# Pairing the half-empty last tiles of two batches, and splitting the first attention block, in a fused attention and MLP-mixer kernel

## The chip, the cores and the metric

The kernel runs on one core of one Trainium2 chip. The metric is the device time of one execution in microseconds (us). Each kernel was executed several times. All executions named here count as fast ones, that is within 1.5% of the fastest of their kernel. A profiled execution also has a span, from its first to its last instruction. It is about 1.8 us shorter than the time of the same execution. Where two traces are compared below, spans are meant. The granted clock is the share of its full speed at which TensorE was clocked, as the profile records it.

Five engines work side by side: PE is TensorE (PEld its weight loads), DVE is VectorE, ACT is ScalarE, POOL is GpSimd and SP is SyncE.

## The reference

There are B = 8 batches of S = 3008 rows. The width D is 256, z is 64 wide, the token layer has 256 hidden units and the channel layer 1536.

```python
# attention with a gate
scores = (1 / S) * z @ z.transpose(0, 2, 1)
x = u * (np.maximum(scores, 0) ** 2 @ v)
# MLP mixer on x: over tokens, then over channels
h  = np.maximum(x.transpose(0, 2, 1) @ w_tok1, 0) @ w_tok2
u2 = x + h.transpose(0, 2, 1)
out = u2 + np.maximum(u2 @ w_ch1, 0) @ w_ch2
```

3008 rows are 23 tiles of 128 rows and one of 64. That last half tile, one in each batch, is what the first part of the change is about.

## The kernel before

A Python program decides the order of the instructions while it builds the kernel. It keeps a model of each engine's time and fills TensorE with pieces of four kinds: score runs (`sc`, z by z), attention blocks (`acc`, squared scores by v), and the heads (`a_ps`, `h_ps`) and tails (`hp`, `op`) of the mixer of the batch before. ScalarE and VectorE empty the accumulators. GpSimd issues the loads of u, v and later z. SyncE issues the transposing DMAs and the stores.

The last layer of the mixer, with the narrow tile, is:

```python
def ch2(q, half, i, end):
    ...
    n = full_tiles[q]
    rows = [P if half * 2 + j < n else TAIL for j in range(2)]   # P = 128, TAIL = 64
    c0 = (half * 2 + i) * P
    for cc in range(CHT):                                        # CHT = 12
        nc.tensor.matmul(
            op[:rows[i], i, :], st["h2", q, cc // 2][:, cc % 2, c0:c0 + rows[i]],
            w_ch2_sb[:, cc, :], start=(cc == 0 and i == 0), stop=(cc == CHT - 1),
            skip_group_check=True)
```

An attention block goes in two halves, each four tiles of keys long, one for each half of the width of v:

```python
def do_half(start, g):
    ...
    dh = blk.half
    count = GK - 1 if g == LAST else GK                          # GK = 4
    start, end = on_pe(start, "full", count * column_time(blk.W))
    for i in range(count):
        av_matmul(blk, g, i, dh, final and i == count - 1)
```

The start loads v chunk 0, then lets GpSimd wait for a late z chunk (`mark`) before it asks for the other v chunks. It turns the first z chunks by matmuls with the identity (`zp`), with matmuls of zeros (`fill`) between them:

```python
load_v(0, 0)
...
nc.gpsimd.tensor_copy(mark[:], zf0[NG - 2][:, 0, :1])
for c in range(1, NG):
    load_v(0, c)
...
fill(6)
for c in range(DT):                     # DT = 2: chunks 0 and 1 on TensorE
    zp = psum.tile([P, GK, P], F32, tag=f"acc{c}", name=f"zp{c}", bufs=1)
    turn_on_pe(double_first_z(c), zp)
    nc.scalar.copy(zTs[0][:, c * GK:c * GK + GK, :], zp[:])
for c in range(DT, GK):                 # chunks 2 and 3 by a transposing DMA
    turn_z(zf0[c], zTs[0], c, nc.vector, "h2", 8)
fill(2)
```

Chunks 4 and 5 are turned later, inside the first block, and ScalarE copies them out.

## Time and profile before

| what | value |
|---|---|
| time, median of 4 runs | 1179.82 us (1178.64 to 1181.26) |
| span of the profiled run | 1179.6 us |
| first matmul starts | 1.2 us |
| first gate of the first block (first `xT<-acc` on VectorE) | 23.95 us |
| last matmul ends | 1175.50 us |
| last matmul to the end of the span | 4.09 us |
| waits of TensorE for a DMA between gate and last matmul | two: 2.08 us at 250 us (`x_sb`), 0.27 us at 491 us (`zT`) |

The prediction was made when three of these four runs were known; their median was 1179.19. It shows the lines of this profile. The last four rows cut the span into three stretches: the start up to the first gate, the middle, which is one stream of matmuls, and the end after the last matmul.

### The profile page before, as it was taken

To read this page: it belongs to the slowest core of one execution; us is meant where nothing else is said; L and a number is where in the kernel's file an instruction comes from. 1 tells how busy PE (TensorE), PEld (TensorE's weight loads), DVE (VectorE), ACT (ScalarE), POOL (GpSimd) and SP (SyncE) were. 2 spreads that over 40 slices of the span, in tenths; PEclk is the share of its full clock that TensorE was granted. 3 is DMA by queue.
4 is the path that set the end of the run, shared out by engine and by line. 5 is a ranking of instruction groups with operands and counts; after the bars stand their busy time and mean duration, and the time that the engine had idled before them with its cause. 6 is when DMAs were issued, how large, how long until landed. Compare 5 with 4: busy or idle time off the path is not lost.

```text
span 1179.6 us, 17778 instructions
## 1 busy us (share of the span) xinstructions
PE 1164.1 (99%) x7023; PEld 635.6 (54%) x7123; DVE 552.0 (47%) x831; ACT 527.7 (45%) x657; POOL 146.8 (12%) x272
## 2 busy tenths in 40 slices
PE   9999999999999999999999999999999999999998
PEld 3334555545546545565555645565454655555666
DVE  5776655245442554434634255233743255412444
ACT  7885644336343453434534345343643345423221
POOL 2561101100121010110101101100201000000000
PEclk9999999999999999999999999999999999999999
DMA  8998957999799985998859977797978989542122
GB/s 147 168 154 138 178 100 134 163 132 164 115 157 172 152 154 107 184 166 147 143 112 184 160 136 131 147 181 136 155 133 144 180 126 165 114 90 63 52 81 61
DMA packets 462339, 162.95 MB, mean 138 GB/s; under 512 B 426224, under 2 KB 439856, under 8 KB 462256
## 3 DMA queue, kind: packets, MB, share of 16 engines
q1 hardware_dynamic: 434400, 129.12, 58.9%
q0 software_dynamic: 27344, 32.32, 20.0%
q8 instruction: 55, 0.90, 0.3%
q10 hardware_dynamic: 512, 0.38, 0.1%
q14 instruction: 28, 0.23, 0.1%
HBM read 65.40 MB, written 24.64 MB: 76 GB/s over the span
## 4 chain that ended last, share of the span: by engine, by line
PE 95%; DMA 2%; issue 1%; SPq 1%; ACT 1%; DVE 1%; POOL 0%; DVEq 0%; POOLq 0%; ACTq 0%
PE acc L497 40%; PE op L708 21%; PE hp L677 20%; PE sc L374 7%; PE a_ps L630 3%; PE h_ps L647 3%; DMA zT<-zr 1%; ACT at L410 1%; DMA x_sb<-xT 1%; PE wp L143 1%; DVE xT L653 0%; SPq L449 0%; SPq L456 0%; POOL zr L111 0%; PE zp L135 0%
## 5 line engine op out<-in xcount | busy, mean ns | idle before, releaser
L410 ACT ACTIVATE at<-sc 128x1024 bf16<-128x1024 f32 (+1 forms) x294 | 281.0, 1022 | 180.0 <-PE sc L374 178.4
L497 PE MATMUL acc<-at,v_sb 128*128 128x512 bf16 (+2 forms) x1474 | 356.1, 378 | 2.4 <-issue 1.0
L497 PEld LDWEIGHTS <-v_sb 128*128 128x128 bf16 (+1 forms) x2304 | 209.0, 98 | 266.4 <-issue 66.0
L690 ACT ACTIVATE h2pre<-hp 128x1024 bf16<-128x1024 f32 (+1 forms) x186 | 186.3, 1006 | 350.5 <-PE hp L677 349.5
L418 DVE TENSOR_TENSOR at<-at 128x1024 bf16<-128x1024 bf16 (+1 forms) x294 | 206.2, 708 | 181.7 <-ACT at L410 181.1
L708 PE MATMUL op<-w_ch_sb,h2pre 128*128 128x256 bf16 (+1 forms) x2304 | 270.3, 273 | 0.1
L677 PE MATMUL hp<-xT,w_ch_sb 128*128 128x512 bf16 (+1 forms) x1118 | 264.1, 374 | 2.2 <-DVE xT L653 0.4
L708 PEld LDWEIGHTS <-h2pre 128*128 128x128 bf16 (+1 forms) x2304 | 225.7, 98 | 48.7 <-issue 1.8
L497 PE MATMUL acc<-fl,v_sb 128*128 128x512 bf16 (+1 forms) x772 | 186.6, 370 | 1.8 <-issue 0.8
L677 PEld LDWEIGHTS <-w_ch_sb 128*128 128x128 bf16 x1152 | 112.4, 98 | 128.3 <-issue 1.9
L721 DVE TENSOR_TENSOR res<-op,u_sb 128x512 f32<-128x512 f32 x88 | 60.9, 692 | 237.5 <-PE op L708 237.1
L692 DVE TENSOR_SCALAR h2pre<-hp 128x1024 bf16<-128x1024 f32 (+1 forms) x102 | 123.0, 1206 | 49.0 <-PE hp L677 48.6
L586 DVE TENSOR_TENSOR xT<-acc,uT 128x512 bf16<-128x512 f32 (+1 forms) x96 | 63.4, 665 | 79.5 <-PE acc L497 79.1
L374 PE MATMUL sc<-zT 64*128 64x512 bf16 (+1 forms) x752 | 97.6, 360 | 0.7 <-DMA zT<-zr 0.3
L398 ACT ACTIVATE at<-sc 128x512 bf16<-128x512 f32 (+3 forms) x164 | 59.4, 446 | 63.7 <-PE sc L374 63.6
L160 POOL DMA_DIRECT2D ur<-in_u_dram x48 | 26.2, 545 | 360.0 <-DMA uT<-ur 360.0
L437 DVE TENSOR_TENSOR at<-at 128x512 bf16<-128x512 bf16 (+3 forms) x164 | 46.0, 333 | 44.3 <-ACT at L398 44.3
L111 POOL COPY zr<-zs 128x512 bf16<-128x512 bf16 x42 | 29.1, 694 | 288.1 <-DMA zT<-zr 287.5
L374 PEld LDWEIGHTS <-zT 64*128 64x128 bf16 x752 | 32.1, 94 | 58.2 <-issue 40.3
L653 DVE TENSOR_TENSOR xT<-xT,h_ps 128x1024 bf16<-128x1024 bf16 (+1 forms) x48 | 55.7, 1191 | 12.2 <-PE h_ps L647 12.2
L149 POOL DMA_DIRECT2D v_sb<-in_v_dram x48 | 26.0, 546 | 186.2 <-PE acc L497 186.1
L630 PE MATMUL a_ps<-x_sb,w_tok_sb 128*128 128x256 bf16 x384 | 44.5, 273 | 2.1 <-DMA x_sb<-xT 2.1
(37 smaller groups left out, 202.0 us busy)
## 6 DMA issues: line engine op xcount, KB each, us to landing
out_dram<-res SPq DMA_DIRECT2D x88, 256.0 KB, 2.3
v_sb<-in_v_dram POOLq DMA_DIRECT2D x40, 256.0 KB, 5.2
ur<-in_u_dram POOLq DMA_DIRECT2D x40, 256.0 KB, 5.6
zs<-in_z_dram POOLq DMA_DIRECT2D x35, 64.0 KB, 4.4
at<-at SPq DMA_TRANSPOSE x123, 2.8
fl<-at SPq DMA_TRANSPOSE x100, 4.6
v_sb<-in_v_dram POOLq DMA_DIRECT2D x8, 192.0 KB, 7.1
w_ch_sb<-in_moe_w_ch_dram POOLq DMA_DIRECT2D x4, 384.0 KB, 5.3
```

The lines of the kernel that those rows point to most:

```text
L374: nc.tensor.matmul(sc[:, r, c0:c1], zT[h, k * P:(k + 1) * P], zT[h, q * QW + c0:q * QW + c1], start=True, stop=True)
L398: nc.scalar.activation(a3[:, i, c0:c1], sc[:, r, c0:c1], ACT.Relu, scale=inv_S)
L410: nc.scalar.activation(view, sv, ACT.Relu, scale=inv_S)
L418: nc.vector.tensor_mul(view, view, view)
L497: nc.tensor.matmul(o, vs[blk.b, g][rows, i, dh * P:(dh + 1) * P], rhs, start=first, stop=stop, skip_group_check=True)
L586: nc.vector.tensor_mul(xT[:, dh, :full * P].rearrange("p (t s) -> p t s", s=P), acc[:, :full * P].rearrange("p (t s) -> p t s", s=P), uT[: ...
L630: nc.tensor.matmul(st["a_ps"][:, th, :], w_tok1_sb[:, k, th * P:(th + 1) * P], x[:, :, i, :], start=(k == 0 and th == 0), stop=(k == KT - ...
L677: nc.tensor.matmul(hp[:, r, :W], w_ch1_sb[:, dc, cc * P:(cc + 1) * P], xT[:, dc, :W], start=(dc == 0), stop=(dc == DT - 1))
L690: nc.scalar.activation(h2[:, :, :W], hp[:, :, :W], ACT.Relu)
L692: nc.vector.tensor_single_scalar(h2[:, :, :W], hp[:, :, :W], 0.0, AX.max)
L708: nc.tensor.matmul(op[:rows[i], i, :], st["h2", q, cc // 2][:, cc % 2, c0:c0 + rows[i]], w_ch2_sb[:, cc, :], start=(cc == 0 and i == 0), s ...
L721: nc.vector.tensor_add(res.rearrange("p i (h d) -> p i h d", d=P), op.rearrange("p i (h d) -> p i h d", d=P), us[:, :, half * 2:half * 2 + ...
```

## The change

The intent is to save TensorE time in two places.

- **Pairs of tails.** The last 64 rows of an even batch wait, as columns of the tile `hs`, for the last 64 rows of the odd batch after it. GpSimd copies both there. One full matmul group then serves both.
- **Start.** The first score run waits for one turned z chunk instead of two. The first two blocks run by half blocks, so that v matmuls can begin when two of the four tiles of `at` are ready. Score runs in the first block may be short when ScalarE would run dry (`starved`). The copies of the late z chunks move from ScalarE to VectorE.

The last batch does its pair tile before its last full tiles (`halves`), so that three adds and three small stores are not at the very end. The core of the diff, with cuts at "...":

```diff
+    def grain(b, q, g):
+        return 2 if b + q == 0 and g < 2 else GK
...
-        dh = blk.half
-        count = GK - 1 if g == LAST else GK
-        start, end = on_pe(start, "full", count * column_time(blk.W))
-        for i in range(count):
-            av_matmul(blk, g, i, dh, final and i == count - 1)
+        dh, tiles = blk.steps[blk.half]
+        start, end = on_pe(start, "full", len(tiles) * column_time(blk.W))
+        for i in tiles:
+            av_matmul(blk, g, i, dh, final and i == tiles[-1])
...
+                if q == NQ - 1:
+                    if c2 == 0 and b % 2 == 0:
+                        pair["hs"] = sb.tile([P, CHT, P], BF16, tag="hs", name="hs", bufs=1)
+                    r = b % 2 * TAIL
+                    nc.gpsimd.tensor_copy(
+                        pair["hs"][:, 2 * c2:2 * c2 + 2, r:r + TAIL], h2[:, :, W - TAIL:W])
...
+            both = half * 2 + i == n
...
+                if both:
+                    h2 = pair["hs"][:, cc, :]
+                else:
+                    h2 = st["h2", q, cc // 2][:, cc % 2, c0:c0 + P]
                 nc.tensor.matmul(
-                    op[:rows[i], i, :], st["h2", q, cc // 2][:, cc % 2, c0:c0 + rows[i]],
-                    w_ch2_sb[:, cc, :], start=(cc == 0 and i == 0), stop=(cc == CHT - 1),
-                    skip_group_check=True)
+                    op[:, i, :], h2, w_ch2_sb[:, cc, :], start=(cc == 0 and i == 0),
+                    stop=(cc == CHT - 1), skip_group_check=True)
...
+        def halves(q):
+            return (1, 0) if (b, q) == (B - 1, NQ - 1) else (0, 1)
+        def pieces_of(q, half):
+            return 1 if q == NQ - 1 and half == 1 and b % 2 == 0 else 2
...
-            "act", end + 0.1, 0.52, 0.66,
-            lambda t: nc.scalar.copy(zTs[0][:, c * GK:c * GK + GK, :], zp[:]),
+            "dve", end + 0.1, 0.66, 0.8,
+            lambda t: nc.vector.tensor_copy(zTs[0][:, c * GK:c * GK + GK, :], zp[:]),
...
-    fill(6)
+    fill(7)
...
-    fill(2)
+    fill(1)
...
+    score_run(units[:2], 5.3)
...
+        elif (starved and now and can_score(done_units, now) == now
+              and has_turned(units[done_units:done_units + now]) <= t + NOW):
+            pick, n_now, ts = "scores", now, t
```

## The prediction

> **What bounds the kernel now.** I began with the page's first part, busy time of each engine, then went to the chain of work that ended last.
>
> ```profile
> PE 1164.1 (99%) x7023; PEld 635.6 (54%) x7123; DVE 552.0 (47%) x831; ACT 527.7 (45%) x657; POOL 146.8 (12%) x272
> PE acc L497 40%; PE op L708 21%; PE hp L677 20%; PE sc L374 7%; PE a_ps L630 3%; PE h_ps L647 3%; DMA zT<-zr 1%; ACT at L410 1%; DMA x_sb<-xT 1%; PE wp L143 1%; DVE xT L653 0%; SPq L449 0%; SPq L456 0%; POOL zr L111 0%; PE zp L135 0%
> ```
>
> TensorE is busy 1164.1 of 1179.6 us, no other engine passes half, and the chain is TensorE nearly from end to end. So the kernel is one long stream of matmuls, and a change counts by the stream time it takes out or by the idle time it closes. There is little idle time: 15.5 us, of which 1.2 lie before the first matmul and 4.1 after the last. Busy time hides two things, though: matmuls that do no work (the fills, L143), and extra spacing inside the stream. So next I took the groups by shape, for the last matmul of the mixer (L708).
>
> ```profile
> L708 PE MATMUL op<-w_ch_sb,h2pre 128*128 128x256 bf16 x2208 | 258.8, 273 | 0.1
> L708 PE MATMUL op<-w_ch_sb,h2pre 128*64 128x256 bf16 x96 | 12.0, 275 | 0.0
> L708 PEld LDWEIGHTS <-h2pre 128*128 128x128 bf16 x2208 | 215.8, 98 | 46.8 <-DVE h2pre L692 0.4 <-ACT h2pre L690 0.3
> L708 PEld LDWEIGHTS <-h2pre 128*64 128x64 bf16 x96 | 9.8, 110 | 1.8 <-issue 1.8
> ```
>
> The last 64 rows of each of the 8 batches take 12 matmuls with 64 weight columns (128*64). Each lasts as long as a full one: half the array is unused and no time is saved. The timeline round the first of them shows more:
>
> ```profile
> 234.49 1.68 PE L497 MATMUL acc<-fl,v_sb 128*128 128x448 bf16 x8
> 236.10 1.50 PE L708 MATMUL op<-w_ch_sb,h2pre 128*64 128x256 bf16 x12
> 237.53 1.69 PE L497 MATMUL acc<-fl,v_sb 128*128 128x448 bf16 x8
> ```
>
> From the first narrow matmul to what follows it are 237.53 - 236.10 = 1.43 us. Reading single start times: full matmuls of this kind follow each other at 109 ns (2101 pairs), the narrow ones at 111, and on entering and on leaving the narrow group the step is about 203 and 205 instead of 109. All eight groups are alike. A narrow group so costs 1.43 + 0.09 = 1.52 us against 12 x 0.109 = 1.31 for a full tile.
>
> Then the start, in the timeline of TensorE:
>
> ```profile
> 4.68 1.53 PE L143 MATMUL wp<-zero 128*128 128x512 bf16 x3
> 6.14 0.85 PE L374 MATMUL sc<-zT 64*128 64x512 bf16 x6
> 6.92 2.33 PE L143 MATMUL wp<-zero 128*128 128x512 bf16 x10
> 9.19 0.82 PE L374 MATMUL sc<-zT 64*128 64x512 bf16 x6
> 9.94 1.90 PE L497 MATMUL acc<-at,v_sb 128*128 128x512 bf16 x8
> 12.68 0.40 PE L135 MATMUL zp<-ident,zr 128*128 128x128 bf16 x4 [0.30 <-DVE zr L129]
> ```
>
> The ten fills at 6.92 are 2.3 us in which the first attention block waits for ScalarE. Then GpSimd's timeline and, for the first issue of that line alone, the view of the tile v_sb:
>
> ```profile
> 8.34 2.66 POOL L149 DMA_DIRECT2D v_sb<-in_v_dram  x5
> ```
>
> ```profile
> DMA to landing us min/median/max: 3.9/3.9/3.9
> ```
>
> These matter for the change: the second chunk of v is issued at 8.34 and lands 3.9 us later, at 12.24. Before, its matmuls begin at about 12.9 and do not meet that limit.
>
> **What the Trainium skill says.** "TensorE: Matmul & The Clock Gate", section Back-to-back issue gap, gives N/2.4 + 2.5 ns for a warm matmul: 109.2 for N = 256, 215.8 for 512. The trace has 109 and 216. The section LDWEIGHTS gives columns/1.2, so 64 columns should load in half the time of 128; here the trace disagrees (110 ns against 98), and the trace decides: narrow tiles gain nothing. The section Why this matters warns of idle gaps over about 3 us, after which the clock falls back. This trace has one wait of 2.08 us (for x_sb, at 250 us) and the matmuls after it run at 216 ns, so a 2 us wait did no harm. "SBUF — State Buffer", section Who interferes with whom, calls the port pair of VectorE and GpSimd an exclusive lock; no row of this trace shows such a block, and the change adds GpSimd copies, so it is a rival below.
>
> **The change part by part.**
>
> *Pairs of tails.* Two batches' 64 rows fill one tile, so 8 narrow groups become 4 full ones. Removed: 8 x 1.52 = 12.2 us, less one exit step of 0.1 for the last group, which nothing follows. Added: 4 x 1.31 = 5.2. Net -6.9 us of stream. The count of 48 matmuls alone would say 48 x 0.109 = 5.2; the rest is the entry and exit steps. All of it lies on TensorE, so all of it should appear in the end.
> Added elsewhere: on GpSimd 48 copies of h2 slices, 4 of u and 4 of xT. The nearest row is a 128x128 copy at 682 ns, so 56 x 0.68 = 38 us on an engine with 1033 us free. VectorE's residual adds stay four per two batches. These lie beside the stream unless a copy is late. In an odd batch the last h2 copy has at least three other tiles (3.9 us) ahead of its use; in the last batch, whose order of halves is turned round, one (1.31 us) plus ten matmuls of its own tile (1.09). It needs about 0.7. No stall.
>
> *The end.* The last matmul is followed now by one add of 128x512 (0.69 us) and one 256 KB store in place of two adds (0.75) and two stores issued one after the other (0.93). Store landings are 2.0 to 2.3 us for either size. I take 0.
>
> *The start.* Fills fall from 19 to 13. The first score run needs one z chunk: one copy on ScalarE (0.5 us) and two cold fills (2 x 0.43) go from in front of it, one fill is put ahead of the turning of z. So scores start at about 1.19 + 7 x 0.43 + 8 x 0.107 + 0.43 = 5.5 instead of 6.14, and half blocks let the first v matmuls begin near 8.0 instead of 9.94. But the instruction order puts the second group of v matmuls straight after, and its first weight load waits for the v chunk of 12.24. TensorE should get there at about 11.5, so 0.8 us are lost there, and more in small waits before.
> Work done when the second group starts: before at 12.9, 8 score pairs, 8 v matmuls, one turned z chunk. After at 12.3, 6 pairs and the rest alike. From there to the end of the first block the order has 5 score runs instead of 3. Each run costs two switches between 64-row and 128-row matmuls: the steps acc to sc and sc to acc are 312 and 308 ns where 216 is the normal one, 0.19 us a run. Further, the turning of the last z chunk waits for its cast on VectorE, which stands behind a square whose ScalarE input comes late: about 0.4. Sum: -0.6 (earlier) + 2 x 0.216 (two pairs) + 2 x 0.19 (switches) + 0.4 = +0.6. With errors in these I take +0.4, from -0.6 to +1.0. The saved fills were not the real limit; the v load takes their place.
>
> *Late z copies on VectorE.* Two copies of 0.6 us leave ScalarE, which has 1.0 and 0.8 us of idle in the same block anyway. Counted in the above, worth nothing of its own.
>
> *Rescheduling.* Shorter mixer work for even batches moves all later pieces. The 2.08 us wait for x_sb may go or stay: -0.4 as a guess between.
>
> Sum: -6.9 + 0.4 + 0.0 - 0.4 = -6.9; 1179.2 - 6.9 = 1172.3 us.
>
> **Rivals.**
> First: the start pays as intended. If the v chunk did not bind, the 2.3 us of waiting fills plus the 0.6 us earlier start would be won less switches, about -2.5 and a time near 1169.5. For it speaks that the change was written for it; against it stands the landing at 12.24, which nothing in the change moves.
> Second: GpSimd becomes a hidden wait. It is in order, and copies now stand between v, u and z loads and behind waits for a DMA transpose (the copy of u for even batches). In the profile GpSimd waits long for freed v buffers (186 us in all, 24.4 at the longest), but always early, and copies come after the points they wait for. A load issued 5 us late still has a block of some 13 us to land. If this fails a few times, +2 to +6: 1175 to 1178.
> Third: narrow tiles were cheaper than I read them and only the 48 matmuls count: 1174.
> Fourth: the 64-row start lets the clock fall back during the new wait near 11 us: +1 to +2. The 2.08 us case speaks against it.
>
> **Range and chances.** The sum is solid in its largest term; the start is uncertain by about 1 us, scheduling by about 1.5, the runs of before spread over 2.6. I say 1172.3, from 1170.0 to 1175.0. A 2% change is 23.6 us, over three times the whole effect: faster 0.01, same 0.98, slower 0.01.
>
> **What would show it.** In the changed profile: no 128*64 group of op; 2256 full ones; four fewer runs of 12; TensorE busy time lower by about 7 to 8 us with a wait of v matmuls (weight load or matmul) of 0.5 to 1.5 us near 11 to 12 us that names DMA v_sb; the first gate of the first block (before at 23.95) between 23.4 and 25.0; no TensorE wait on GpSimd. I am wrong if that gate comes 1.5 us or more earlier, if hs appears among the waits of TensorE, or if the end lies outside 1170 to 1175.

## The result and the profile after

The changed kernel took 1172.12 us (median of 4 runs, 1171.72 to 1176.86) against 1179.82 for the kernel before. The ratio is 0.9943, with a 95% interval from 0.9915 to 0.9972: under the 2% line, so "the same", and 1172.3 had been predicted. Ratios here are the mean time of one kernel's fast runs over that of the other's in the same rounds, so they are not quite the ratio of the medians quoted beside them.

The busy time and the chain of work that ended last, from the page of the changed kernel:

```profile
PE 1162.0 (99%) x7069; PEld 630.4 (54%) x7069; DVE 557.6 (48%) x836; ACT 523.4 (45%) x652; POOL 159.9 (14%) x328
PE acc L513 42%; PE op L748 21%; PE hp L707 21%; PE sc L379 7%; PE a_ps L653 4%; PE h_ps L670 3%; ACT at L417 1%; DMA zf<-in_z_dram 0%; DMA v_sb<-in_v_dram 0%; DVE xT L676 0%; DVE at L425 0%; DVE h2pre L722 0%; DVE xT L606 0%; SPq L120 0%; DVE res L760 0%
```

The chain is TensorE as before; the links `DMA x_sb<-xT` and `DMA zT<-zr`, 1% each, are gone and a short link to `v_sb` is new. Read the first line with care. TensorE's busy time fell by 2.1 us only, although the span fell by 9.5. The reason is in the counts. After, matmuls and weight loads are both 7069. Before, 7123 weight loads stood beside 7023 matmuls: a hundred matmul records are missing in that trace, and their time is missing from its busy sum. Busy times of these two traces cannot be subtracted; start times can.

The groups by shape of the last layer:

```profile
L748 PE MATMUL op<-w_ch_sb,h2pre 128*128 128x256 bf16 x2208 | 258.4, 273 | 0.3 <-DVE xT L676 0.2
L748 PE MATMUL op<-w_ch_sb,hs 128*128 128x256 bf16 x48 | 5.9, 273 | 0.0
```

The 96 narrow matmuls (128*64) are gone, and 48 full ones that read `hs` have come. The timeline of TensorE round a pair tile, to be read against the narrow tile in the prediction:

```profile
378.49 0.93 PE L513 MATMUL acc<-fl,v_sb 128*128 128x448 bf16 x4
379.25 1.47 PE L748 MATMUL op<-w_ch_sb,hs 128*128 128x256 bf16 x12
380.56 0.92 PE L513 MATMUL acc<-fl,v_sb 128*128 128x448 bf16 x4
```

From the first matmul to what follows it are 380.56 - 379.25 = 1.31 us for two batches' rows, where one batch's had taken 1.43 and an entry step.

The start, in the timeline of TensorE (start, length, what, count, and in brackets the idle time before it and what ended that):

```profile
5.52 0.61 PE L379 MATMUL sc<-zT 64*128 64x512 bf16 x4
...
7.79 1.47 PE L513 MATMUL acc<-at,v_sb 128*128 128x512 bf16 x6
...
10.84 0.40 PE L135 MATMUL zp<-ident,zr 128*128 128x128 bf16 x4 [0.51 <-DVE zr L129]
11.69 1.04 PE L513 MATMUL acc<-at,v_sb 128*128 128x512 bf16 x4 [0.45 <-DMA v_sb<-in_v_dram]
```

The scores begin at 5.52 instead of 6.14 and the first v matmuls at 7.79 instead of 9.94. But the second group of v matmuls waits for its data until 11.69. That chunk of v was issued at 7.68, in GpSimd's timeline:

```profile
7.68 2.65 POOL L149 DMA_DIRECT2D v_sb<-in_v_dram  x5
```

Its landing took 4.0 us (to 11.64 in the trace), and TensorE goes on within 0.05 us of it. What the earlier start had won is lost by the end of the block, as the first gate shows in VectorE's timeline, of the kernel before and of the changed one:

```profile
23.95 1.28 DVE L586 TENSOR_TENSOR xT<-acc,uT 128x512 bf16<-128x512 f32 x2
```

```profile
23.91 1.28 DVE L606 TENSOR_TENSOR xT<-acc,uT 128x512 bf16<-128x512 f32 x2
```

The end became longer, from 4.09 us after the last matmul to 4.66. The closing instructions of the queues, in the view of the program's last line (count, shortest/median/longest in ns, first and last start), before and after:

```profile
L1007 POOLq DRAIN  x3: 45/102/7825, 1046.2 to 1179.3; - x3
```

```profile
L1071 POOLq DRAIN  x3: 45/102/7917, 1161.1 to 1169.5; - x3
L1071 SPq DRAIN  x3: 7/7/7, 1168.6 to 1169.3; - x3
```

GpSimd closes with a drain (its closing instruction) of some 7.9 us whose record begins together with its last own instruction. Before, that was at 1046 us, long hidden. After, the record begins at 1161.08, the last copy of `hs` runs from 1161.10 to 1161.40, and the drain ends near 1169.0, when SyncE's drain, behind the last store, has been ready since 1168.6.

The account of the two traces, start to start, in us:

| stretch | before | after | difference |
|---|---|---|---|
| to the first gate | 23.95 | 23.91 | -0.04 |
| waits for a DMA in the middle | 2.35 | 0 | -2.35 |
| the rest of the middle, up to the last matmul | 1149.19 | 1141.51 | -7.68 |
| after the last matmul | 4.09 | 4.66 | +0.57 |
| span | 1179.6 | 1170.1 | -9.5 |

So the traces differ by 9.5 and the medians by 7.7. The experiments were made to tell what of this belongs to the change.

### The profile page after: what moved, and what is told of

The parts are those of the page before. It is cut to its first block, busy times and chain, and to the rows that moved or that the text cites. A ratio compares the mean times of both kernels' runs of the same rounds, so it can differ in the third digit from the quotient of the medians.

```text
span 1170.1 us, 17839 instructions
## 1 busy us (share of the span) xinstructions
PE 1162.0 (99%) x7069; PEld 630.4 (54%) x7069; DVE 557.6 (48%) x836; ACT 523.4 (45%) x652; POOL 159.9 (14%) x328
## 4 chain that ended last, share of the span: by engine, by line
PE 97%; DMA 1%; DVE 1%; ACT 1%; issue 1%; SPq 0%; POOL 0%; DVEq 0%; ACTq 0%
PE acc L513 42%; PE op L748 21%; PE hp L707 21%; PE sc L379 7%; PE a_ps L653 4%; PE h_ps L670 3%; ACT at L417 1%; DMA zf<-in_z_dram 0%; DMA v_sb<-in_v_dram 0%; DVE xT L676 0%; DVE at L425 0%; DVE h2pre L722 0%; DVE xT L606 0%; SPq L120 0%; DVE res L760 0%
## 5 line engine op out<-in xcount | busy, mean ns | idle before, releaser
L720 ACT ACTIVATE h2pre<-hp 128x1024 bf16<-128x1024 f32 (+1 forms) x183 | 183.6, 1007 | 303.0 <-PE hp L707 300.3
L748 PE MATMUL op<-w_ch_sb,h2pre 128*128 128x256 bf16 x2208 | 258.4, 273 | 0.3 <-DVE xT L676 0.2
L748 PEld LDWEIGHTS <-h2pre 128*128 128x128 bf16 x2208 | 215.9, 98 | 46.2 <-issue 0.5
L513 PE MATMUL acc<-fl,v_sb 128*128 128x512 bf16 (+1 forms) x800 | 190.7, 371 | 0.2 <-DVE xT L606 0.2
L722 DVE TENSOR_SCALAR h2pre<-hp 128x1024 bf16<-128x1024 f32 (+1 forms) x105 | 126.5, 1205 | 54.3 <-PE hp L707 54.1
L111 POOL COPY zr<-zs 128x512 bf16<-128x512 bf16 x42 | 26.5, 632 | 294.0 <-DMA zT<-zr 293.6
L670 PE MATMUL h_ps<-w_tok_sb,a_sb 128*128 128x512 bf16 (+1 forms) x192 | 44.4, 374 | 0.1
```

The lines of the kernel that those rows point to most:

```text
L513: nc.tensor.matmul(o, vs[blk.b, g][rows, i, dh * P:(dh + 1) * P], rhs, start=first, stop=stop, skip_group_check=True)
L670: nc.tensor.matmul(h[:, dh, :W], st["a"][:, th, dh * P:(dh + 1) * P], w_tok2_sb[:, th, q * QW:q * QW + W], start=(th == 0), stop=(th == 1))
L720: nc.scalar.activation(h2[:, :, :W], hp[:, :, :W], ACT.Relu)
L722: nc.vector.tensor_single_scalar(h2[:, :, :W], hp[:, :, :W], 0.0, AX.max)
L748: nc.tensor.matmul(op[:, i, :], h2, w_ch2_sb[:, cc, :], start=(cc == 0 and i == 0), stop=(cc == CHT - 1), skip_group_check=True)
```

## The experiments

The theory on entering them was that of the prediction: the pairs of tails pay about 7 us, the start nothing because the arrival of v takes the place of the fills, and the x_sb wait is not the change's doing. The rivals were that the start pays something too, that only the 48 matmuls count and not the steps round narrow groups, and that the order of work had removed the x_sb wait. A second question was what lengthened the end. All runs gave correct results. The kernels came in three groups of rounds. The kernel before ran along in each: 1182.89 us median in the first (11 runs), 1182.05 in the second (12 runs, of which 11 are those of the first) and 1178.92 in the third (11). On the chip of the first two its runs spread from 1178.64 to 1188.85, which makes those ratios loose. For that reason the stretches of the traces are given beside the times.

### One part alone: the pairs, the start, and the kernel before once more

e1_pairs_only takes the start hunks out of the changed kernel:

```diff
-        return 2 if b + q == 0 and g < 2 else GK
+        return GK
...
-            "dve", end + 0.1, 0.66, 0.8,
-            lambda t: nc.vector.tensor_copy(zTs[0][:, c * GK:c * GK + GK, :], zp[:]),
+            "act", end + 0.1, 0.52, 0.66,
+            lambda t: nc.scalar.copy(zTs[0][:, c * GK:c * GK + GK, :], zp[:]),
...
-    fill(7)
+    fill(6)
...
-    fill(1)
+    fill(2)
...
-    score_run(units[:2], 5.3)
...
-        starved = blk is not None and blk.b + blk.q == 0 and (
+        starved = False and blk is not None and blk.b + blk.q == 0 and (
```

> The pairs of tails and the turned end alone, with the old start. Theory (the pairs are all of the gain, the start is worth nothing): 8 narrow groups of 1.52 us go and 4 full ones of 1.31 us come, -6.9 us, and the end loses about 0.5 us; the ratio to before is 0.993 to 0.995, like the whole change; the first gate of the first block comes at 23.95 us as before. Rival A (the start carries a good part): only -4 to -5 us, ratio 0.996. Rival B (the x_sb wait of 2.1 us near 250 us went away by luck of that one execution and not by the new order): the wait is back in this trace. If the order did it, this trace has no such wait, since the order round the second batch's token matmuls is the new one.

e2_start_only puts the same hunks, in the other direction, into the kernel before: half blocks, the one-chunk score run, the z copies on VectorE, and no pairs.

```diff
+        return 2 if b + q == 0 and g < 2 else GK
...
+            blk.steps = [(dh, tiles[i:i + n]) for i in range(0, GK, n) for dh in range(DT)]
...
-            "act", end + 0.1, 0.52, 0.66,
+            "dve", end + 0.1, 0.66, 0.8,
...
+    score_run(units[:2], 5.3)
```

> The new first block alone, with the narrow tails of before. Theory: the second group of v matmuls waits for its v chunk near 11.7 us, two more score runs cost 0.19 us each, so the first gate stays within 0.4 us of 23.95 and the time within 1 us of before, ratio 0.999 to 1.001. Rival (the start pays as it was meant to): gate at 22.5 or earlier, time 1.5 to 2.5 us less, ratio 0.998 or lower. The x_sb wait near 250 us should be seen here as before if it belongs to the old order of the mixer.

e4_before_again is the kernel before, unchanged (the diff is empty), for a second trace of it.

> The kernel before, unchanged, for the noise and for the x_sb wait. Ratio 1.000 with an interval that says what can be told apart (I expect 0.998 to 1.002). If the wait of 2.1 us for x_sb near 250 us belongs to the program, it is here again at 1.5 us or more; if it was chance, it is gone or at another place.

Measured, with the kernel before at 1182.89 in the same rounds (stretches in us; "middle" is from the first gate to the last matmul without its waits for a DMA, which are in the next column):

| kernel | time, median | ratio, 95% | gate | middle | waits | end |
|---|---|---|---|---|---|---|
| e1_pairs_only | 1173.49 | 0.9925, 0.9899 to 0.9951 | 23.66 | 1141.67 | 2.10 | 4.66 |
| e2_start_only | 1180.87 | 0.9998, 0.9965 to 1.0031 | 24.02 | 1148.89 | 0 | 4.10 |
| e4_before_again | 1179.61 | 0.9978, 0.9952 to 1.0005 | 24.02 | 1149.04 | 0.99 | 4.07 |

The pairs alone bring the whole gain, and the start alone nothing that can be seen. The waits of TensorE, in the view of waits (in all, times, longest), of e4_before_again and of e1_pairs_only, settle the x_sb wait:

```profile
PE a_ps L630 <- DMA x_sb<-xT: 1.0, 1, 1.0
```

```profile
PE a_ps L653 <- DMA x_sb<-xT: 2.1, 1, 2.1
```

The unchanged kernel has 2.08 us of it in one execution and 0.99 in the next, and the pairs bring back all of it. It is a transfer that comes early or late from one execution to another. So the 2.08 us that the first pair of traces shows as gained is not a gain of the change. Nor is the 0.27 us for `zT`, which e2_start_only, e4_before_again and e7_wide_tails don't have either.

### The shape of the narrow tile without its pair

e7_wide_tails keeps the eight last tiles of the kernel before, but makes them 128 columns wide. GpSimd copies 64 columns beside the real ones, and their results are not stored. The number of matmuls stays, only the width changes.

```diff
+                if W < QW:
+                    nc.gpsimd.tensor_copy(h2[:, :, W:], h2[:, :, W - TAIL:W])
...
-                    op[:rows[i], i, :], st["h2", q, cc // 2][:, cc % 2, c0:c0 + rows[i]],
+                    op[:, i, :], st["h2", q, cc // 2][:, cc % 2, c0:c0 + P],
```

> The kernel before, with its 64-row tails computed as full 128-column tiles (the 64 h2 columns are put beside themselves by a GpSimd copy, the upper 64 result rows are not used), not paired: the same number of matmuls as before. Theory (a narrow group costs 0.2 us over its matmuls for entering and leaving): 8 x 0.2 = 1.6 us less than before, and in the trace each such group takes 1.31 us from its first matmul to what follows, with no step of 203 or 205 ns. Rival (only the 48 matmuls count): the time as before, and the steps stay, as they belong to the change of output or tile.

It took 1177.81 us, ratio 0.9974 (0.9943 to 1.0005). The first of the tiles in TensorE's timeline:

```profile
234.97 1.68 PE L497 MATMUL acc<-fl,v_sb 128*128 128x448 bf16 x8
236.48 1.47 PE L710 MATMUL op<-w_ch_sb,h2pre 128*128 128x256 bf16 x12
237.79 1.68 PE L497 MATMUL acc<-fl,v_sb 128*128 128x448 bf16 x8
```

237.79 - 236.48 is 1.31 us, as for any full tile. Its middle is 1147.19 us. The three traces with narrow tiles (before, e4_before_again, e2_start_only) have 1149.19, 1149.04 and 1148.89, on the mean 1149.04. So the width alone is worth -1.85; eight times the difference of 1.52 and 1.31 would be -1.7. The time alone would not tell (its interval reaches 1.0005); the steps and the middle do. The rival in which only the 48 matmuls count falls. The kernels with pairs have 1141.51 (after), 1141.67 (e1_pairs_only), 1141.70, 1141.85 and 1141.38 (the runs e3, e11 and e9 below), on the mean 1141.62; e3b, below, has 1141.59. From e7_wide_tails to them are -5.6, where 48 matmuls of 0.109 make -5.2.

### Is the start bound by v?

e3_v_early issues v chunk 1 directly behind chunk 0, at the head of GpSimd's queue, and not after the late z chunk.

```diff
     load_v(0, 0)
+    load_v(0, 1)
...
-    for c in range(1, NG):
+    for c in range(2, NG):
         load_v(0, c)
```

> The changed kernel with the second chunk of v asked for before the wait for the late z, right behind the first chunk. Theory (in the changed start the v chunk that lands at 11.7 us is the wait that took the place of the fills): no wait of v matmuls on v, the second group starts about 0.4 us earlier, near 11.25, just behind the turning of z; first gate at 23.5 (0.4 earlier than 23.91). Not more, because the turning of z itself waits 0.5 us for its cast on VectorE. Rival (the v chunk does not matter, the switches and casts do): gate stays at 23.9. Risk: the v load delays the z chunks, then the gate comes later, 24.2 or more, with TensorE waiting for zT. In the end time the difference is too small to see.

e3b_v_early_pool_casts does that too, and makes the casts of the late z chunks (`zr`) early on GpSimd, so that VectorE's queue does not delay them.

```diff
-        nc.vector.tensor_copy(zr[:], zf0[c].unsqueeze(2).to_broadcast([P, GK, 2, d_qk]))
+        engine = nc.vector if c < GK else nc.gpsimd
+        engine.tensor_copy(zr[:], zf0[c].unsqueeze(2).to_broadcast([P, GK, 2, d_qk]))
...
+    load_v(0, 1)
...
-    for c in range(1, NG):
+    load_v(0, 2)
+    zr_late = {c: double_first_z(c) for c in range(GK, NG)}
+    for c in range(3, NG):
         load_v(0, c)
...
-        zr = double_first_z(c)
-        free["dve"] = max(free["dve"], pe[0]) + 0.45
+        zr = zr_late.pop(c)
```

> As e3_v_early, and the casts of the two late z chunks go to GpSimd, issued before the later v chunks, so that the turning of z stands behind no square on VectorE. Theory: both waits that I name for the start (v chunk 0.45 us, casts 0.5 and 0.25 us) are gone, the second group of v matmuls starts near 10.7, the gate comes at 22.8, 1.1 us before that of the changed kernel. Rival: other waits come in (the later v chunks, issued 1.5 us later, or ScalarE), and the gate stays above 23.5.

e3_v_early took 1172.92 us (ratio 0.9935, 0.9892 to 0.9978) and e3b_v_early_pool_casts 1172.95 (0.9939, 0.9891 to 0.9987): neither differs from the changed kernel. TensorE's timeline of e3_v_early:

```profile
10.10 0.61 PE L379 MATMUL sc<-zT 64*128 64x512 bf16 x4 [0.16 <-DMA zT<-zr]
...
11.35 1.03 PE L513 MATMUL acc<-at,v_sb 128*128 128x512 bf16 x4
```

and of e3b_v_early_pool_casts:

```profile
8.48 1.47 PE L514 MATMUL acc<-at,v_sb 128*128 128x512 bf16 x6 [0.58 <-DMA v_sb<-in_v_dram]
...
10.77 0.61 PE L380 MATMUL sc<-zT 64*128 64x512 bf16 x4 [0.82 <-DMA zT<-zr]
```

In the first, the wait at 11.7 is gone and the v matmuls start 0.34 us sooner. But the score run that stood at 9.19 stands at 10.10, because the turned z chunk arrives later now. The first gate comes at 23.57, 0.34 us earlier than in the changed kernel. In the second, v chunk 0 and z both come late, and the gate is at 24.07. There VectorE also did a square first, although the last matmuls of the block were done. The gain of about a microsecond that a pure v limit promised is not there. Asking for v earlier makes z later: the first z chunk that a DMA turns lands at 10.05, 10.72 and 10.83 us in the three traces with the early load (these two and e10_both below), and at 8.39 to 9.14 in the ten others.

What binds can be read from the landings in all traces. In the six with the changed start and the late load of v, the second group of v matmuls begins 0.05 us after its chunk has landed (at 11.24 to 12.03), and the gate follows 12.22 or 12.23 us after the group's start. So in these the landing of v sets the gate, and its scatter is the gate's. In the four traces with the old start that group begins 0.6 us or more after the landing, and the gate follows about 11.0 us after the group's start (the record of the group's first matmul is missing in these traces and was put 0.216 us before the next). So the prediction's limit was right for the changed kernel. It was too narrow as a cause: with v early the limit passes to z, and the gates, 23.57, 24.07 and 24.30, lie among those of the six with the late load, 23.51 to 24.30.

### What lengthened the end

Two theories were open. By one, the turned order of the last batch hides less than it should. By the other, GpSimd is still busy when the others are done.

e5_end_order_back undoes the turned order, so the pair tile is the last one:

```diff
-            return (1, 0) if (b, q) == (B - 1, NQ - 1) else (0, 1)
+            return (0, 1)
```

> The changed kernel with the old order of halves in the last chunk, so that the pair tile is last. The trace of before has 4.09 and 4.07 us from the last matmul to the end of the span, the changed kernel 4.66 and 4.66 (with the pairs alone). Theory A (the turned order costs the 0.6 us, a 128x512 add and store at the end instead of small ones): back to 4.1, time 0.5 us less. Theory B (three adds and three stores at the end are worse, the turn was right for the pair tile): 5.0 or more. Theory C (the length of the end is not set by the stores but by where the program ends): 4.66 stays.

It took 1175.66 us (ratio 0.9945, 0.991 to 0.998), and its end is 5.02 us after the last matmul. So the turned order is right; it is worth 0.36 in this pair of traces. Here the last stores set the end: SyncE is ready only 3.96 us after the last matmul, and GpSimd's drain has ended at 3.58. Most of the profiled execution's extra time, 1176.9 us of span against 1170.1, is of another kind. These are its waits for transfers:

```profile
PE acc L513 <- DMA v_sb<-in_v_dram: 4.2, 4, 2.7
...
PE sc L379 <- DMA zT<-zr: 2.3, 1, 2.3
```

Leaving out the start, these are 5.9 us in the middle that the changed kernel's own trace does not have, with the same order up to the last batch. They are the scatter of transfers again.

e8_copies_eightfold repeats each copy into `hs` eight times, to see how much slack GpSimd's copies have:

```diff
-                    nc.gpsimd.tensor_copy(
-                        pair["hs"][:, 2 * c2:2 * c2 + 2, r:r + TAIL], h2[:, :, W - TAIL:W])
+                    for _ in range(8):
+                        nc.gpsimd.tensor_copy(
+                            pair["hs"][:, 2 * c2:2 * c2 + 2, r:r + TAIL], h2[:, :, W - TAIL:W])
```

> The changed kernel with each of the 48 GpSimd copies of h2 made eight times (the same copy, 0.3 us each). Theory (the copies lie beside the stream with room to spare): 48 x 7 x 0.3 = 100 us more GpSimd work, and the time within 1 us of the changed kernel but for the last chunk, where the pair tile's last copy then comes 2.4 us instead of 0.3 us after its h2: matmuls of the pair tile wait about 1 to 2 us there. Rival (GpSimd is near the path already: loads or h2 buffers come late): 5 us or more, with waits of TensorE on hs, v_sb or freed h2 buffers all through the run.

It took 1183.43 us, ratio 1.0018 (0.9983 to 1.0053). The view of waits of TensorE, and then the end of its timeline:

```profile
PE op L749 <- POOL hs L728: 8.0, 4, 2.3
```

```profile
1166.16 0.39 PE L749 MATMUL op<-w_ch_sb,hs 128*128 128x256 bf16 x2 [2.17 <-POOL hs L728]
1168.90 0.61 PE L749 MATMUL op<-w_ch_sb,hs 128*128 128x256 bf16 x2 [2.35 <-POOL hs L728]
1171.64 0.61 PE L749 MATMUL op<-w_ch_sb,hs 128*128 128x256 bf16 x2 [2.13 <-POOL hs L728]
1172.04 5.33 PE L749 MATMUL op<-w_ch_sb,h2pre 128*128 128x256 bf16 x24
```

Of 48 groups of copies, 44 stayed hidden although they were eight times as long. Three of the four waits lie in the last chunk, and one of 1.38 us at 672 us. I had expected 1 to 2 us of loss and missed the size twice. The last `h2` chunks come faster than eight copies of 0.3 us each, so the delays add up instead of overlapping. And the clock follows: the last 24 matmuls take 5.33 us where the changed kernel's take 2.78. The same stretch in the view of windows (length, then busy time and count of each engine, the granted clock, the DMA share and GB/s):

```profile
1166.00:1172.00 6.00, 1.36 (x6) 0.53 (x7) 0.00 (x0) 0.00 (x0) 4.73 (x17) 0.61 0.00 0
```

The granted clock was 0.61 in these 6 us. What the run says of the change itself: the single copies, eight times shorter, are far from being late except in the last chunk. And the end of this kernel is 3.98 us, not 4.66, because here the last copies lie so long before the last matmul that GpSimd's drain ends 1.8 us after it; in the changed kernel it ends 3.58 us after it, when SyncE has been ready since 3.21. That is what the second theory asks for.

The last three kernels went together on another chip.

e11_after_again is the changed kernel, unchanged (the diff is empty).

> The changed kernel, unchanged, on the same chip as the two others. First gate at 23.9 and 4.66 us from the last matmul to the end if these belong to the program; waits of matmuls on DMA (v, z, x_sb) anywhere from 0.4 to 6 us if these are chance, as the other traces suggest. Time about 1172 to 1173.

e9_end_off_pool takes the last batch's copies from GpSimd. The engine that empties `hp` writes the 64 columns to `hs` itself, in a second instruction:

```diff
+                if (b, q) == (B - 1, NQ - 1):
+                    hs = pair["hs"][:, 2 * c2:2 * c2 + 2, TAIL:]
+                    V = W - TAIL
+                    if on_act:
+                        nc.scalar.activation(h2[:, :, :V], hp[:, :, :V], ACT.Relu)
+                        nc.scalar.activation(hs, hp[:, :, V:W], ACT.Relu)
+                    else:
+                        nc.vector.tensor_single_scalar(h2[:, :, :V], hp[:, :, :V], 0.0, AX.max)
+                        nc.vector.tensor_single_scalar(hs, hp[:, :, V:W], 0.0, AX.max)
+                    return
```

> The changed kernel, but in the last chunk of the last batch ScalarE and VectorE write the pair tile themselves instead of GpSimd copies. In the traces GpSimd's closing drain takes 7.92 us after its last copy and ends 3.58 us after the last matmul in the changed kernel, when SyncE is ready at 3.21; in e8, where it ended at 1.8, the end was 3.98. Theory: without late copies the end is 4.0 us (0.7 less), against 0.1 to 0.2 us more before the last tiles for the split evacuation; time 0.5 us less than the changed kernel. Rival (the drain is idle waiting for the others and not a cause): the end stays at 4.66.

e10_both is e9_end_off_pool with the early load of v chunk 1 as well:

```diff
+                if (b, q) == (B - 1, NQ - 1):
+                    hs = pair["hs"][:, 2 * c2:2 * c2 + 2, TAIL:]
...
+    load_v(0, 1)
...
-    for c in range(1, NG):
+    for c in range(2, NG):
```

> e9_end_off_pool and e3_v_early together, the candidate to beat the changed kernel. First gate at 23.6, end at 4.0: 1.0 us less than the changed kernel by these two numbers, 1171.2 against 1172.2; in the total this may drown in the DMA waits that come and go from run to run.

Measured, with the kernel before at 1178.92 in the same rounds:

| kernel | time, median | range | ratio, 95% | gate | waits in the middle | end |
|---|---|---|---|---|---|---|
| e11_after_again | 1172.28 | 1171.98 to 1175.72 | 0.9947, 0.9935 to 0.9959 | 24.30 | 1.34 + 1.73 | 4.66 |
| e9_end_off_pool | 1172.03 | 1170.74 to 1175.98 | 0.9946, 0.9933 to 0.9959 | 23.51 | 0 | 3.98 |
| e10_both | 1174.78 | 1171.0 to 1178.2 | 0.9958, 0.994 to 0.9976 | 24.30 | 1.88 | 3.98 |

The closing drain of e9_end_off_pool:

```profile
L1081 POOLq DRAIN  x3: 45/93/7908, 1101.0 to 1168.6; - x3
```

It starts at 1101 instead of 1161, and the end is 3.98 us, 0.68 less than 4.66. So the late copies on GpSimd are what lengthens the end. How they do it is shown for about half. Their drain holds back the closing instructions from 3.21 us after the last matmul, when SyncE is ready, to 3.58. The other 0.3 us is a pause between two of GpSimd's closing instructions, from 4.20 to 4.55 us after the last matmul; in e9_end_off_pool they follow each other within 0.07. The drain does not always bring this pause. e7_wide_tails copies late on GpSimd too, its drain also ends at 3.58, and its end is 4.36 without the pause; e5_end_order_back has the pause, although its drain is not the last to end. What makes the pause is not shown.

In the time the 0.68 cannot be told from the scatter (1172.03 against 1172.28), so e9_end_off_pool is better by its trace only. Its lowest run, 1170.74, is the lowest of all runs here.

e11_after_again shows the v wait larger than in the first trace of the same kernel:

```profile
12.07 1.04 PE L513 MATMUL acc<-at,v_sb 128*128 128x512 bf16 x4 [1.21 <-DMA v_sb<-in_v_dram]
```

The v chunk was issued at 8.23 here and at 7.68 there, since GpSimd issues it after a z chunk has landed. The gate is at 24.30.

e10_both has no gain from the early v load: v chunk 0 came late, with a wait of 1.3 us at 7.6. It has a second loss too, in the timeline of TensorE:

```profile
625.74 2.76 PE L513 MATMUL acc<-fl,v_sb 128*128 128x512 bf16 x12
...
630.92 0.39 PE L379 MATMUL sc<-zT 64*128 64x512 bf16 x2 [1.88 <-DMA zT<-zr]
...
632.19 4.36 PE L707 MATMUL hp<-xT,w_ch_sb 128*128 128x512 bf16 x12
```

Twelve matmuls of the same size take 2.76 us before the wait of 1.88 and 4.36 soon after it, and the granted clock over 620 to 640 us was 0.91. That is 1.6 us more. The middle of this trace without its wait is 1143.25 us, which is also 1.6 above the mean of the other five with pairs.

## Why the prediction was right

The time was right within 0.2 us, but that is partly luck of the medians: the fourth run of the kernel before raised its median from 1179.19 to 1179.82, so a predicted 6.9 stands beside a measured 7.7 here and beside 6.6 in the third group of rounds. The steps fared as follows.

- **Pairs of tails, -6.9: right, a little small.** Between the traces with narrow tiles and those with pairs the middle differs by 1149.04 - 1141.62 = 7.4 us. The two groups spread over 0.3 and 0.5, so the excess of 0.5 is about as large as the spread. The waits for VectorE in the middle (0.4 us before, 0.4 after) do not account for it; it stays unexplained. The steps on entering and leaving a narrow group, which the first reading of "48 fewer matmuls" leaves out, were confirmed by e7_wide_tails.
- **GpSimd's copies, hidden: right, and cheaper than assumed.** There is no wait of TensorE on GpSimd in the changed kernel. The copies took 304 ns on the mean and not 682, as the group of them shows:

```profile
L727 POOL COPY hs<-h2pre 128x128 bf16<-128x128 bf16 x48 | 14.1, 304 | 128.3 <-ACT h2pre L720 109.2 <-DVE h2pre L722 19.0
```

  The price had been taken from a single copy before, which was no good sample: one of these 48 took 684 too.
- **The end, 0: wrong by 0.6.** The adds and stores were counted rightly: SyncE is ready 3.2 us after the last matmul, against 3.3 before. What failed is the account of the end as one add and one store. It left out GpSimd's closing drain of 7.9 us, which was in the trace before, at 1046 us, where it cost nothing. The drain holds the end back by 0.37 us; the pause of 0.3 that goes with it here is not explained.
- **The start, +0.4 (-0.6 to +1.0): right within its range.** With the old start the gate came at 23.95, 24.02, 23.66 and 24.43 (before, e4, e1, e7), on the mean 24.02. With the new start it came at 23.91, 24.02, 24.30, 23.51, 23.92 and 24.11 (after, e2, e11, e9, e5, e8), on the mean 23.96. The start is worth 0, give or take 0.3. The fills fell from 19 to 13 as said, and the wait for v stands where it was put. Against 0.5 to 1.5 us it was 0.45 before the matmul and 0.6 before its weight load in the first trace, 1.21 before the matmul in e11_after_again and 0.37 to 0.41 in the four others. The sum can be checked term by term: the later costs were put at 1.2 us, and from the second group of v matmuls to the gate it is 12.2 us instead of 11.0. But that group came 1.2 us earlier (11.69 against 12.9) and not 0.6, so the two cancel. One sub-step failed. The landing of that chunk "which nothing in the change moves" does move, by itself: its issue came at 7.32 and at 8.34 in two executions of the kernel before. The prediction had taken the later one for fixed. That is chance in the loads: the landings spread from 11.35 to 12.28 us with the old start and from 11.24 to 12.03 with the new one. And the cause is wider than v (e3_v_early).
- **The x_sb wait, -0.4 as a guess: not an effect.** It was 2.08, 0.99 and 0 with the old mixer order and 2.10, 1.67 (e3b), 1.34 and 0 with the new one. Together with the waits for `zT` at 630 us and for `v_sb` near 95 us it adds up to 0 to 5.9 us in the traces of kernels that otherwise agree in their middle within 0.6. The guess between "stays" and "goes" was the right thing to do with one trace.
- **The signs to look for.** No 128*64 group, 2256 full matmuls, the gate between 23.4 and 25.0 and no wait on `hs` all came true. "TensorE busy time lower by 7 to 8 us" did not: it fell by 2.1, because a hundred matmul records are missing in the trace of before. The 7023 beside 7123 in the first line that the prediction quotes could have warned me.
- **The rivals.** That the start pays (1169.5) falls to e2_start_only. That GpSimd becomes a hidden wait falls in the form it had; it took part at the very end only. That only the matmuls count (1174) falls to e7_wide_tails. That the clock falls back during the new wait was not seen: the mean clock of the changed kernel's trace is 1.000. But e8 and e10 show that the danger was real. The port pair of VectorE and GpSimd was called a rival and then not listed, and the reading that no row shows such a block was wrong. In the trace of before 20 squares on VectorE took over a fifth longer than is usual for their size, up to 1.87 us where 0.69 is usual, and all 20 overlapped a copy on GpSimd. VectorE was not the limit, so this cost nothing that can be seen, and the new copies into `hs` added none of it: only one square met one of them, and took 0.68 us.

The sum of what was measured is -7.4 for the pairs, 0 for the start and +0.6 for the end, so -6.8 against the -6.9 predicted: errors of 0.5 and 0.6 in opposite directions nearly cancelled, and a start term and a guess of 0.4 each had cancelled in the sum already.

## What to carry to other kernels

In this kernel a leftover tile that filled half the array cost as much as a full one and a further 0.2 us for getting in and out, so leftovers of independent pieces are worth packing together. Filler work or idle time at the start is worth removing only up to the next thing that binds, here the arrival of the data, so look first for the landing of what is used next. Before moving small work to an idle engine late in a program, look at what that engine still has to do after its last instruction; and compare traces from start to start, and an unchanged kernel with itself, before giving a wait to the change.

## What the Trainium skill lacked or had wrong

- "TensorE: Matmul & The Clock Gate", section LDWEIGHTS, scales the load with the columns. That formula, taken by itself, does not fit: here 64 columns took 110 ns and 128 took 98, and a matmul with 64 weight columns took as long as a full one (275 and 273 ns).
- The same page, section Back-to-back issue gap, gives about 131 ns for each matmul of N = 512 in a sustained stream of loads and matmuls, and calls 216 the figure of an isolated one. In the stream of this kernel they follow each other at 216 ns.
- "TensorEngine Tiling (Array Packing)", section Key Properties, says that a change of the tiling mode drains TensorE, but not for how long. Here the step into a group of 64 columns was 203 ns and out of it 205 where 109 is normal; between 64-row and 128-row matmuls of N = 512 the steps were 312 and 308 where 216 is normal.
- "TensorE: Matmul & The Clock Gate", section Why this matters for your kernels, warns of idle gaps over about 3 us. Here one wait of 1.88 us (e10_both) was followed by a granted clock of 0.91 over 20 us and a loss of about 1.6 us, and three of 2.1 to 2.4 us by 0.61; but one of 2.08 (the kernel before) and even one of 2.70 (e5_end_order_back, at 95 us) left it at 1.00. So gaps under 3 us were not always harmless, and these runs do not show what decides.
- "VectorE: DVE Perf Modes", section The DRAIN you can't avoid, speaks of drains from the beginning and the end of every program, on all five engines, of a constant 12 ns or so. GpSimd's closing drain took 7.8 to 7.9 us in all thirteen traces, counted from the start of its last instruction, and where that instruction came late it held the end of the program back by 0.37 us. No page says that GpSimd ends so.
